# Where the last four scale sums of the opening are made: on VectorE, or on GpSimd and ScalarE

## The chip, the core and the metric

The kernel runs on one core of one Trainium2 chip. The metric is the device time of one execution in microseconds (us). The engines are named as in the profile: PE is TensorE (PEld its weight loads), DVE is VectorE, ACT is ScalarE, POOL is GpSimd, SP is SyncE, whose queue issues the DMAs.

## The reference

One transformer-like block on x (2048 tokens x 1024 channels, f32), modulated by a condition vector c:

```
mod = (silu(c) @ w_mod) in six rows of 1024: sa, ca, ga, sb, cb, gb
h = layernorm(x) * (1 + ca) + sa
x = x + ga * infini_attention(h)      # 32 heads, 4 segments of 512 tokens, wq wk wv wo, memory
h = layernorm(x) * (1 + cb) + sb
x = x + gb * token_mlp(h)             # layernorm, w1 (2048 -> 3584), gelu, w2 (3584 -> 2048)
```

The change touches only how ca, the first scale row, is summed: ca[n] is the sum over k of silu(c)[k] * w_mod[k, 1024 + n].

## The kernel before, in words

The work has four stages: an opening (the first 53 us or so), the attention over 64 steps of (pass, group of four heads, segment), the output projection with the second modulation, and the token MLP in two large products of matrices. Matmuls with f32 accuracy are made as three products of a high part (a cast, L123 or L125) and a low part (the rest, L126), both held in one "page".

The opening works on segment 0 and goes over eight chunks `ct` of 128 channels (lines 278 to 298). Each chunk needs a shift column sa and a scale column 1 + ca, which stand per partition in the tile `saca`. For both, a tile `wm` (128 x 1024) of w_mod is loaded (L281, eleven buffers). The shift's tile is transposed in memory beforehand, so that silu(c), spread over all partitions in `scb`, is multiplied along the free axis and summed by one VectorE operation with an accumulator (L283). The scale's tile is treated in two ways. For chunks 0 to 3 (`NSC = 4`) it lies untransposed and eight small matmuls with one column each sum it on TensorE (L291). For chunks 4 to 7 it lies transposed as the shift's does; two GpSimd products of 512 columns (L287) write wm times scb in place and one ScalarE copy with an accumulator sums it (L288). VectorE then adds 1 (L295).

With both columns, `h_chunk` makes the chunk of h: four TensorE transposes of the normalised x tiles into a PSUM bank (L223), a ScalarE evacuation with scale and shift (L225), a high part (on ScalarE for segment 0, L123; on VectorE for later segments, L125) and a low part (on GpSimd for segment 0, on GpSimd or VectorE for later ones, L126). `first_chunk` multiplies the finished page by the first weights (L196 for k and v, twelve matmuls; L204 for q, three), one chunk behind `h_chunk`.

Beside it, segment 1 is prepared: its four x tiles are queued on SP behind the last `wm` (`issue_after(last_wm)`, L573), VectorE takes their statistics (L131) and ScalarE normalises them (L218). Then come the evacuation of the first products (L358 to L366), segment 1's eight `h_chunk`s (line 577), and the projections of the second step (lines 578 to 581). From there on each step's pieces are laid out by the loop of lines 630 to 653.

What sets the order: the program's text gives each engine's instructions, but the order on each engine is planned at build. Line 1053 asks the tile framework to schedule with a timed simulation of the program, so the durations it assumes for the operations enter into the order. The profile shows that order: saca of chunk 4 stands ahead of saca of chunk 3 on VectorE (L295, both near 35.5 us), and the matmuls with high parts stand ahead of those with low parts on TensorE. Each engine then runs its list in that order, waiting by semaphores. Tiles of the opening share memory with tiles of later stages, which wait for their release.

Of the kernel before, what the change touches and what calls it, by code (L numbers as in the profile page):

```python
# [12 lines left out]
AF = mybir.ActivationFunctionType  # L13
ALU = mybir.AluOpType
# [33 lines left out]
def attention_and_mlp(ctx, tc, x, wq, wkv, wo, beta, w1, b1, w2, b2, c, wm_a, wm_b, out):  # L48
    nc = tc.nc
    V, A, G, T, SY = nc.vector, nc.scalar, nc.gpsimd, nc.tensor, nc.sync  # L50
# [18 lines left out]
    scb, gaw = (a.tile([P, D], F32, name=n) for n in ("scb", "gaw"))  # L69
# [94 lines left out]
    def load_part(g, pr, kind, part, res):  # L164

        if pr == 0:
            split_part(g, kind, part, fetch_part(g, kind, part))
            return
        for i in range(2):
            w = aw.tile([P, 2, 512], F32R, tag="w", bufs=8, name=f"w{kind}{pr}_{g}_{part}_{i}")  # L170
            SY.dma_start(w.bitcast(F32), wsp[g, 2 * part + i if kind == "v" else 4 + i])
            res[kind, 2 * part + i] = w
# [47 lines left out]
    def h_chunk(pool, xs, seg, ct):  # L220
        ps = bank(*(("s1", 2), ("s2", 2))[ct % 2] if seg else ("s2", 2), f"hps{seg}_{ct}")
        for i in range(4):
            T.transpose(ps[:, 128 * i:128 * i + 128], xs[i][:, P * ct:P * ct + P], ident)  # L223
        h32 = pool.tile([P, L], F32, tag="h32", bufs=HB, name=f"h32_{seg}_{ct}")
        A.activation(h32, ps, AF.Identity, scale=saca[:, ct, 1:2], bias=saca[:, ct, 0:1])  # L225
        pg = new_page(f"h{seg}_{ct}")
        split(pg, h32, V if seg else A, V if seg and ct % 2 else G)
        hpages[seg, ct] = pg
# [38 lines left out]
    def first_chunk(ct):  # L267
        h = hpages[0, ct]
        for half in range(2):
            kv_chunk(W[0, 0], h, half, ct, two_tiles(first[half]))  # L270
        q_chunk(W[0, 0], h, ct, first[2])
# [5 lines left out]
    scs = s1p.tile([P, NK], F32, name="scs")  # L277
    for ct in range(NK):
        for part in range(2):
            wm = s1p.tile([P, D], F32, tag="wm", bufs=11, name=f"wm{ct}_{part}")  # L280
            last_wm = SY.dma_start(wm, wm_a[part, ct])  # L281
            if part == 0:
                V.scalar_tensor_tensor(wm, wm, 1.0, scb, op0=ALU.mult, op1=ALU.mult, accum_out=saca[:, ct, 0:1])  # L283
            elif ct >= NSC:
                for i in range(2):
                    c = slice(512 * i, 512 * i + 512)
                    G.tensor_tensor(wm[:, c], wm[:, c], scb[:, c], op=ALU.mult)  # L287
                A.activation(wm, wm, AF.Copy, accum_out=scs[:, ct:ct + 1])  # L288
            else:
                for k in range(NK):  # L290
                    T.matmul(scale_ps[:, ct:ct + 1], wm[:, P * k:P * k + P], sc[:, k:k + 1], start=(k == 0),  # L291
                             stop=(k == NK - 1), skip_group_check=True)
        if ct < 3:
            load_part(0, 0, *(("v", 0), ("q", 0), ("v", 1))[ct], W[0, 0])
        V.tensor_scalar_add(saca[:, ct, 1:2], (scale_ps if ct < NSC else scs)[:, ct:ct + 1], 1.0)  # L295
        h_chunk(s1p, xs[0], 0, ct)
        if ct:
            first_chunk(ct - 1)
# [331 lines left out]
    for n in range(-LEADS, 4 * NI + VL):  # L630
# [11 lines left out]
        if 59 <= m < 67:  # L642
            seg, ct = 2 + (m - 59) // 4, 2 * ((m - 59) % 4)
            reload_h(seg, ct)
            reload_h(seg, ct + 1)
        if 4 * NI - 5 <= m < 4 * NI + 3:
            i = m - 4 * NI + 5
# [409 lines left out]
```

## Time and profile before

| | us |
|---|---|
| median of three runs | 2281.92 (2280.88 to 2282.4) |
| the profiled execution | 2281.25 |
| its span, first to last instruction | 2279.5 |
| mean granted TensorE clock | 0.989 of full speed |

| engine | busy in the first 54 us | busy in the span |
|---|---|---|
| PE | 39.63 | 2214.7 |
| DVE | 33.70 | 1671.9 |
| ACT | 32.76 | 1148.1 |
| POOL | 32.03 | 735.6 |

How to read the lines that follow. A timeline row has start, duration, engine, line, operation, output tile, input tiles, shapes and count; in brackets stand the idle time ahead of it and what ended it. A row of the chain of waits has start, duration, engine, tile and line. A row of the waits has who waited for whom, then the total, the number of times and the longest. A row of a group ends with busy time, mean nanoseconds of one, and idle time ahead by releaser. A row of one tile's or line's instructions has minimum, median and maximum duration in nanoseconds, and the first and last start. A row of a window has the stretch, its length, the busy time and the count of PE, PEld, DVE, ACT and POOL, then the granted TensorE clock (1.00 is full), the DMA engines' share and GB/s.

### The profile page before, as it was taken

The page shows a single profiled execution, that of the slowest core. Times are in us where ns is not written, and L with a number is a line of the kernel's source. Part 1 is how long each engine was busy: PE and PEld are TensorE (multiplying, and loading weights), DVE is VectorE, ACT ScalarE, POOL GpSimd, SP SyncE. Part 2 cuts the span into 40 slices and gives each one's busy share as a digit, 9 for nine tenths or more (in the row PEclk, how much of TensorE's full clock was granted, in tenths as well). Part 3 has the DMA queues.
Part 4 walks back from the last instruction along what each step waited for, and adds up shares of the span by engine and source line. Part 5 has one row for each costly group of instructions (what it writes and reads, how often), then busy time and mean ns, then how long its engine had stood idle before and what let it go on. Part 6 is the DMA issues. An engine that isn't in the chain of part 4 may idle for free.

```text
span 2279.5 us, 38372 instructions
## 1 busy us (share of the span) xinstructions
PE 2214.7 (97%) x13802; PEld 1905.5 (84%) x13802; DVE 1671.9 (73%) x3798; ACT 1148.1 (50%) x2090; POOL 735.6 (32%) x843
## 2 busy tenths in 40 slices
PE   7999999999999999999999999999999999999999
PEld 6888898888988889987877887888887888888887
DVE  6676677766777677664878555788889787878787
ACT  6476677665666666654646333533334242424232
POOL 5165566655766666644000000023333000000000
PEclk9999999999999999999999999999999999999999
DMA  6656565687567566673455765556557441414134
GB/s 259 202 170 172 145 192 167 188 265 230 167 189 209 171 193 185 210 245 108 138 197 201 273 239 194 218 198 235 208 203 277 162 153 56 153 56 143 56 120 148
DMA packets 172882, 415.72 MB, mean 182 GB/s; under 512 B 17268, under 2 KB 71572, under 8 KB 163732
## 3 DMA queue, kind: packets, MB, share of 16 engines
q1 hardware_dynamic: 172692, 413.27, 55.3%
q8 instruction: 110, 1.80, 0.3%
q14 instruction: 80, 0.66, 0.1%
HBM read 237.28 MB, written 125.06 MB: 159 GB/s over the span
## 4 chain that ended last, share of the span: by engine, by line
PE 80%; DMA 7%; DVE 7%; ACT 3%; POOL 2%; issue 1%; SPq 0%; DVEq 0%; ACTq 0%; POOLq 0%
PE mx L849 39%; PE nps L196 13%; PE qps L204 8%; PE po L734 6%; PE pv L504 4%; DMA xb<-x1d 2%; DMA x1e<-xb 2%; PE a L475 1%; PE sx L440 1%; PE sz L440 1%; PE rd L412 1%; DMA sk<-nt 1%; PE a L478 1%; DVE xb L906 1%; PE up L422 1%
## 5 line engine op out<-in xcount | busy, mean ns | idle before, releaser
L849 PE MATMUL mx<-bU,sp 128*128 128x512 f32 x2352 | 535.4, 389 | 3.0 <-DVE sp L126 1.7
L849 PEld LDWEIGHTS mx<-bU,sp 128*128 128x128 f32 x2352 | 441.0, 188 | 96.9 <-DVE sp L126 2.7
L123 ACT CAST sp<-wr 128x384 fp32r<-128x384 f32 (+2 forms) x408 | 217.0, 545 | 451.7 <-PE mx L849 373.7
L196 PE MATMUL nps<-wv,h 128*128 128x256 f32 x3072 | 436.5, 283 | 3.5 <-POOL h L126 3.5
L849 PE MATMUL mx<-bA,sp 128*128 128x512 f32 x1764 | 434.4, 392 | 5.5 <-ACT sp L123 3.3
L490 POOL TENSOR_TENSOR ph<-p,ph 128x640 f16<-128x640 f32 x256 | 377.3, 1495 | 153.7 <-ACT ph L488 153.5
L196 PEld LDWEIGHTS nps<-wv,h 128*128 128x128 f32 x3072 | 404.5, 190 | 10.4 <-POOL h L126 4.7
L849 PEld LDWEIGHTS mx<-bA,sp 128*128 128x128 f32 x1764 | 332.9, 189 | 76.4 <-ACT sp L123 4.4
L126 DVE TENSOR_TENSOR sp<-wr,sp 128x384 fp32r<-128x384 f32 (+2 forms) x408 | 258.1, 643 | 32.0 <-ACT sp L123 31.9
L856 DVE TENSOR_TENSOR ac<-mx,ac 128x512 f32<-128x512 f32 x280 | 189.3, 685 | 92.8 <-PE mx L849 92.3
L204 PE MATMUL qps<-h,wq 128*128 128x512 f32 x768 | 199.9, 406 | 2.3 <-DVE pv L507 1.1
L734 PE MATMUL po<-wo,ots 128*128 128x512 f32 x768 | 183.8, 395 | 6.6 <-DVE more_x L737 2.8
L488 ACT CAST ph<-p 128x1280 f16<-128x1280 f32 x128 | 161.2, 1260 | 44.7 <-POOL p L486 44.1
L734 PEld LDWEIGHTS po<-wo,ots 128*128 128x128 f32 x768 | 144.3, 190 | 38.0 <-ACT ots L123 2.7
L441 DVE CUSTOM_DVE_ANT_0 sx<-sx,mask 128x128 f32<-128x128 f32 (+1 forms) x256 | 109.8, 429 | 86.5 <-PE sx L440 85.1
L204 PEld LDWEIGHTS qps<-h,wq 128*128 128x128 f32 x768 | 144.0, 194 | 31.3 <-issue 2.8
L849 PE MATMUL mx<-bB,sp 128*128 128x512 f32 x588 | 164.0, 389 | 0.0
L486 POOL TENSOR_SCALAR_AFFINE_SELECT p<-p 128x256 f32<-128x256 f32 x256 | 119.5, 475 | 125.3 <-ACT p L479 65.9
L504 PE MATMUL pv<-vp,ph 128*128 128x97 bf16 (+1 forms) x2560 | 144.1, 203 | 1.6 <-DVE red L511 1.3
L504 PEld LDWEIGHTS <-ph 128*128 128x128 f16 x2560 | 115.3, 99 | 25.4 <-issue 12.9
L849 PEld LDWEIGHTS mx<-bB,sp 128*128 128x128 f32 x588 | 110.5, 188 | 23.1
L856 DVE TENSOR_TENSOR cc<-mx,cc 128x512 f32<-128x512 f32 x140 | 94.2, 682 | 37.5 <-PE mx L849 37.2
(208 smaller groups left out, 3208.3 us busy)
## 6 DMA issues: line engine op xcount, KB each, us to landing
sk<-sg SPq DMA_DIRECT2D x384, 128.0 KB
wr<-in_w_dram SPq DMA_DIRECT2D x28, 1024.0 KB
wr<-in_w_dram SPq DMA_DIRECT2D x32, 768.0 KB
bstu<-ucd SPq DMA_DIRECT2D x28, 768.0 KB
wsp<-wv SPq DMA_DIRECT2D x32, 512.0 KB
rawm<-in_wm_b_dram SPq DMA_DIRECT2D x32, 512.0 KB
wv<-wsp SPq DMA_DIRECT2D x32, 512.0 KB
pcd<-cc SPq DMA_DIRECT2D x14, 1024.0 KB
```

Of the source, the lines that this page charges most:

```text
L123: A.copy(hi, src)
L126: lo_eng.tensor_tensor(lo, src, hi.bitcast(F32), op=ALU.subtract)
L196: T.matmul(ps[:, aa], h[:, j, 128 * tt:128 * tt + 128], wt[:, i, o:o + 256], start=(n == 0), stop=(n >= 6 * NK - 2), skip_group_check=True)
L204: T.matmul(ps, wt[:, i, o:o + 128], h[:, j], start=(k + n == 0), stop=(3 * k + n == 3 * NK - 1))
L441: marks[4 * t + h - LEADS, "V"] = V.tensor_tensor_reduce(o, o, mask[:, 384 - 128 * i:], 1.0, -3.0e38, op0=ALU.add, op1=ALU.max, accum_out= ...
L486: G.affine_select(w, w, pattern=[[0, 2], [1, 128]], compare_op=ALU.is_ge, fill=0.0, base=0, channel_multiplier=-1)
L488: marks[n, "A"] = A.copy(ph[:, 0], p32)
L490: marks[n, "G"] = G.tensor_tensor(ph[:, 1, c], p32[:, c], ph[:, 0, c], op=ALU.subtract)
L504: T.matmul(pv[:, i, 0:w], ph[:, part, o:o + 128], d["vp"][:, j, h, 0:w], start=(n == 0), stop=(n == 19), skip_group_check=True)
L734: T.matmul(ps, os_[:, i, P * ct:P * ct + P], wop[ct, nh][:, j], start=(n == 0), stop=(n == 3 * NK - 1))
L849: T.matmul(ps, ops[q][:, i, P * k:P * k + P], b[:, j], start=(m == 0 and first), stop=(m == 3 * nk - 1), skip_group_check=True)
L856: V.tensor_tensor(d, ps, d, op=ALU.add)
```

## The change

For chunks 4 to 7, the two GpSimd products and the ScalarE sum are replaced by one VectorE operation that multiplies and sums, in the form that the shift sums have. Loads, layouts, buffers and everything behind `scs` stay.

```diff
             elif ct >= NSC:
-                for i in range(2):
-                    c = slice(512 * i, 512 * i + 512)
-                    G.tensor_tensor(wm[:, c], wm[:, c], scb[:, c], op=ALU.mult)
-                A.activation(wm, wm, AF.Copy, accum_out=scs[:, ct:ct + 1])
+                V.scalar_tensor_tensor(wm, wm, 1.0, scb, op0=ALU.mult, op1=ALU.mult, accum_out=scs[:, ct:ct + 1])
```

## The prediction

> **What bounds the kernel now.** First the page's engine shares, then what PE waited for in the opening (28 to 72 us), then the chain of waits through that stretch, then the timelines of single engines.
>
> ```profile
> PE 2214.7 (97%) x13802; PEld 1905.5 (84%) x13802; DVE 1671.9 (73%) x3798; ACT 1148.1 (50%) x2090; POOL 735.6 (32%) x843
> ```
>
> PE is busy 97% of the span, so work taken off POOL or ACT in the steady part gives nothing. The opening differs. The waits of PE there:
>
> ```profile
> PE nps L196 <- POOL h L126: 3.5, 4, 1.4
> PE hps L223 <- ACT x L218: 0.8, 1, 0.8
> PE hps L223 <- ACT h L225: 0.8, 1, 0.8
> PE hps L223 <- DVE sg L126: 0.7, 1, 0.7
> PE kps L372 <- DVE r L365: 0.4, 1, 0.4
> ```
>
> The largest is four waits for POOL's low part of an h page. The chain says why POOL is late:
>
> ```profile
> 31.70 5.00 POOL wm L287 x4
> ...
> 37.20 1.73 POOL h L126
> ...
> 42.40 1.23 POOL h L126
> 43.63 2.49 POOL wm L287 x2
> 46.12 1.24 POOL h L126
> ...
> 47.40 1.21 PE nps L196 x8
> ...
> 53.32 0.34 ACT k L358
> ...
> 55.02 1.13 ACT x L218
> ```
>
> From 31.7 to 47.4 us the chain alternates between the h pages' low parts and the products that the change removes (L287); only at 47.4 does PE take it over, until the last first_chunk ends at 53.3. Then ACT's evacuation follows, and with it the last normalised x tile of segment 1 (55.02). PE's own rows:
>
> ```profile
> 38.99 1.19 PE L196 MATMUL nps<-wv,h 128*128 128x256 f32 x8 [0.23 <-POOL h L126]
> ...
> 43.68 1.21 PE L196 MATMUL nps<-wv,h 128*128 128x256 f32 x8 [1.45 <-POOL h L126]
> ...
> 47.40 1.21 PE L196 MATMUL nps<-wv,h 128*128 128x256 f32 x8 [1.34 <-POOL h L126]
> ...
> 49.62 1.11 PE L196 MATMUL nps<-wv,h 128*128 128x256 f32 x8
> ...
> 51.73 1.11 PE L196 MATMUL nps<-wv,h 128*128 128x256 f32 x8
> ...
> 56.21 0.55 PE L223 MATMUL hps<-ident,x 128*128 128x128 f32 x3 [0.84 <-ACT x L218]
> ```
>
> Chunks that don't wait are 51.73 - 49.62 = 2.1 us apart; those that wait lose 0.23, 1.45 and 1.34.
>
> **What goes and what comes.** The groups of the stretch 28 to 54 us, all engines:
>
> ```profile
> L287 POOL TENSOR_TENSOR wm<-wm,scb 128x512 f32<-128x512 f32 x8 | 11.0, 1407 | 0.0
> ...
> L225 ACT ACTIVATE h<-hps,saca 128x512 f32<-128x512 f32 x6 | 4.5, 771 | 3.9 <-DVE saca L295 3.9
> L288 ACT ACTIVATE wm<-wm 128x1024 f32<-128x1024 f32 x4 | 4.2, 1058 | 6.7 <-POOL wm L287 6.7
> L123 ACT CAST h<-h 128x512 fp32r<-128x512 f32 x6 | 3.6, 616 | 0.1
> ...
> L134 ACT ACTIVATE mv<-mv,eps 128x1 f32<-128x1 f32 x4 | 1.2, 290 | 0.3 <-DVE mv L133 0.3
> ...
> L135 ACT ACTIVATE mv<-mv 128x1 f32<-128x1 f32 x4 | 0.8, 198 | 0.1
> ```
>
> POOL loses eight products, 11.0 us. ACT loses four sums, 4 x 1.06 = 4.2 us, and the short reads behind them. DVE gains four operations like those of the shift sums, whose price and surroundings are these:
>
> ```profile
> L283 DVE SCALAR_TENSOR_TENSOR wm<-wm,scb x8: 1209/1216/2284, 12.7 to 38.3; 128x1024 f32<-128x1024 f32 x8
> ```
> ```profile
> 29.38 1.22 DVE L283 SCALAR_TENSOR_TENSOR wm<-wm,scb 128x1024 f32<-128x1024 f32 x1
> 30.53 0.08 DVE L283 DVE_READ_ACCUMULATOR wm<-wm,scb 128x1 f32 x1
> 35.44 0.15 DVE L295 TENSOR_SCALAR saca<-scs 128x1 f32<-128x1 f32 x1 [4.83 <-ACT wm L288]
> ```
>
> One takes 1.22 us alone and up to 2.28 beside POOL. I take 4 x 1.22 = 4.9 us of DVE time; the bounds are 4.9 and 4 x 2.28 = 9.1. I take the low end because what stretched them was POOL's two-input work, most of which goes. The cover is DVE's idle 4.83 us ahead of 35.44, where it waits for ACT's sum of chunk 4: that wait is itself a part of what goes.
>
> [...]
>
> **Does DVE become late instead?** Of the tiles for chunks 4 to 7, six operations remain after 30.6 us (two shift sums, four scale sums): 6 x 1.22 = 7.3 us, ending at 37.9. The data are there in time:
>
> ```profile
> 28.00:38.00 10.00, 10.00 (x69) 9.47 (x68) 4.97 (x10) 4.83 (x8) 7.59 (x6) 1.00 1.02 408
> 38.00:48.00 10.00, 6.97 (x49) 5.81 (x48) 6.51 (x17) 7.30 (x17) 10.00 (x8) 1.00 0.18 70
> ```
>
> The transfers end near 38 + 10 x 70/408 = 39.7 us, and the four x tiles queued behind the last wm take 4 x 0.524 MB at 408 GB/s = 5.1 us, so the last wm lands at about 34.6 (an estimate from these two rows). The SP queue issues the same loads from the same buffers in the same order; the last five wait for tiles of chunks 0 to 2, which the change leaves alone. No DMA is added. After saca of chunk 7 come 0.77 + 0.62 us on ACT and 1.2 to 1.3 on POOL (the chain's 1.23 and 1.24). With PE's transposes at 37.0 as now, ACT is through chunks 4 to 7 at 38.1 + 4 x 1.39 = 43.7 and POOL at 45.0, while PE reaches the low part of chunk 7 at 51.73 - 3.0 = 48.7. Even with all six at 2.28 us, DVE ends at 44.3 and POOL's page is ready near 47.2. So PE is late next, with its own 2.1 us a chunk.
>
> **The sum.** *Term 1*, PE's three waits for POOL: 0.23 + 1.45 + 1.34 = 3.0 us; the end of the chunks goes from 53.3 to 50.3. Bounds 0 and 3.5 (with the fourth wait, the rest of that row of waits).
>
> *Term 2*, the last x tile of segment 1 (ACT, 55.02 to 56.15). The segment's own operations:
>
> ```profile
> L131 DVE BATCH_NORM_STATS2 st<-x x8: 637/678/683, 39.9 to 48.6; 128x6 f32<-128x512 f32 x8
> L218 ACT ACTIVATE x<-x,mv x4: 1227/1228/1273, 49.8 to 54.9; 128x1024 f32<-128x1024 f32 x4
> ```
>
> Behind 38.1 ACT has 5.6 us for h pages, four normalisations at 1.23 and 1.2 + 0.8 of small operations (L134, L135): 12.5 us, so it could finish near 50.6, 0.3 us behind the chunks' end where it is now 2.85 behind. What else waits there (the 0.8, 0.7 and 0.4 of the first fence) stays, since it follows the evacuation. I take the 1.1 us of the chain's own piece; bounds 0 and 2.7 (0.84 + 0.82 + 0.66 + 0.42, all four).
>
> *Term 3*, the clock:
>
> ```profile
> 53.30:58.00 4.70, 2.78 (x21) 1.90 (x18) 1.87 (x4) 4.70 (x12) 1.82 (x8) 1.00 0.00 0
> 58.00:62.00 4.00, 3.18 (x17) 3.12 (x17) 3.72 (x6) 3.68 (x7) 1.28 (x1) 0.57 0.67 141
> ```
>
> After the thin stretch (PE 2.78 of 4.7 us) TensorE is granted 0.57 for 4 us: 0.43 x 4 = 1.7 us lost. With less waiting the spell may shorten or go; bounds 0 and 1.7, and I take the middle, 0.9.
>
> Sum 3.0 + 1.1 + 0.9 = 5.0 us off the profiled execution's 2281.25: **2276.2 us**. (That execution is 0.67 below the median of 2281.92 and inside the three runs.) All bounds together: 0 to 7.9 us, 2273.3 to 2281.25. Behind the opening PE is full (452 of 460 us in a row below), so what is won stays unless the later order changes.
>
> **The rivals.** *The gate stays at x.* DVE has the four new operations ahead of segment 1's statistics (L131). If the order fixed at build puts the statistics as late as now, or POOL's remaining low parts stretch them, the last x tile still ends near 56 and the 3.0 us of term 1 become waiting for it. For it: DVE starts these statistics between 39.9 and 48.6 now, and DVE alone gets more work. Against it: DVE idles 4.83 us ahead of 35.44 for ACT's sum, and is busy only 6.51 of the 10 us from 38 to 48. Time 2280.5; it decides if the last L218 ends later than about 55.
>
> *The order of later work turns out worse (slower).* The order on each engine is fixed at build by a timed plan, so other costs in the opening can reorder work far behind it. What an order is worth shows in two stretches of the same attention work:
>
> ```profile
> 100.00:540.00 440.00, 420.21 (x3591) 379.97 (x3590) 303.87 (x898) 299.25 (x560) 260.76 (x302) 0.96 0.63 187
> 540.00:1000.00 460.00, 452.15 (x4012) 414.03 (x4011) 322.52 (x1003) 291.83 (x518) 304.61 (x372) 1.00 0.64 188
> ```
>
> The first loses 19.8 us idle and 0.04 x 440 = 17.6 us of clock, the second 7.9 and almost none. The losses come in spells of half clock:
>
> ```profile
> 132.00:142.00 10.00, 9.69 (x41) 7.74 (x40) 7.25 (x21) 8.62 (x15) 6.47 (x9) 0.66 0.90 277
> 258.00:268.00 10.00, 7.60 (x22) 5.93 (x23) 6.82 (x21) 5.18 (x10) 5.38 (x5) 0.66 0.27 107
> ```
>
> A spell costs 0.34 x 10 + 0.31 = 3.7 us in the first row and 0.34 x 10 + 2.40 = 5.8 in the second, mean 4.75. One more cancels the gain; three more give 2276.2 + 14.3 = 2290.5. It decides from two more spells on. For it: the first stretch, with several spells, begins close behind the opening. Against it: a shift of everything by the same few microseconds keeps the order, and a spell may as well vanish (one fewer: 2276.2 - 4.75 = 2271.5).
>
> [...]
>
> **How the numbers follow.** 0.2% is 4.6 us, about what a measurement of this kernel can tell from no change: under 2277.4 is faster, over 2286.5 slower. Forecast 0.50 (0.42 of it faster, 0.08 within the bound, where term 2 or 3 fails); the gate at x 0.20, within the bound; the later order 0.30 (0.28 slower, 0.02 within). Together faster 0.42, same 0.30, slower 0.28. The likeliest case alone spans 2273 to 2279. The range reaches down to all bounds won and a spell less at the cheap price (2273.3 - 3.7 = 2269.6) and up to the later order: **2270 to 2291**.
>
> **What would show it.** Right: no wait of PE for POOL's h pages between 38 and 50 us; the last saca of the opening near 38, ahead of the statistics; the last first_chunk near 50.3; the last L218 near 51; the shift of 4 to 5 us still there at 100, 540 and 1000 us. Term 1 is wrong if PE waits there for DVE or ACT instead; term 2 if hps still waits for x; term 3 if the granted clock behind 55 is as low for as long. The sum as a whole is wrong if the shift at 100 us is right and the one at 1000 us isn't.

## The result, and the profile after

The changed kernel takes 2297.6 us (median of six runs, 2294.36 to 2301.1) against 2282.15 us for the kernel before beside it: ratio 1.0067, 95% interval 1.0055 to 1.008, so 15 us slower. The forecast was 2276.2 us, within 2270 to 2291. The profiled execution has a span of 2295.5 us, 16.0 more than before. In the changed kernel's profile every line behind the change has a number that is 3 lower.

First TensorE's waits and rows of the opening, the counterparts of those shown for before:

```profile
PE up L419 <- DVE pk L390: 2.0, 1, 2.0
PE hps L223 <- ACT x L218: 1.5, 2, 1.2
PE nps L196 <- POOL h L126: 0.7, 2, 0.3
```
```profile
41.83 1.21 PE L196 MATMUL nps<-wv,h 128*128 128x256 f32 x8 [0.35 <-POOL h L126]
...
47.57 1.55 PE L196 MATMUL nps<-wv,h 128*128 128x256 f32 x12
48.95 0.85 PE L204 MATMUL qps<-h,wq 128*128 128x512 f32 x3
...
52.83 0.55 PE L223 MATMUL hps<-ident,x 128*128 128x128 f32 x3 [1.25 <-ACT x L218]
...
57.54 2.10 PE L419 MATMUL up<-v,pk 128*128 128x132 f32 x8 [1.99 <-DVE pk L390]
...
70.29 4.39 PE L196 MATMUL nps<-wv,h 128*128 128x256 f32 x35 [0.34 <-POOL h L126]
```

The waits for POOL fell from 3.5 to 0.7 us, and the last first_chunk ends at 49.8 us instead of 53.3. But the lead is gone twenty microseconds later: TensorE waits 1.25 us for a normalised x tile and 1.99 for `pk`, and the last low part of segment 1 reaches it at 70.29 us, where it was 69.21 before.

The four new operations cost what the rows of before said:

```profile
L285 DVE SCALAR_TENSOR_TENSOR wm<-wm,scb x4: 1215/1215/1224, 29.2 to 39.4; 128x1024 f32<-128x1024 f32 x4
```

So the opening accounts for 1 us of the 16. The other 15 are lost further on, most of them hundreds of microseconds behind the change. Before, then after, in two stretches of the attention:

```profile
100.00:600.00 500.00, 478.78 (x4114) 434.32 (x4113) 345.94 (x1028) 338.68 (x630) 296.63 (x346) 0.97 0.64 189
600.00:1000.00 400.00, 393.59 (x3489) 359.68 (x3488) 280.44 (x875) 252.40 (x448) 268.74 (x329) 1.00 0.63 186
```
```profile
100.00:600.00 500.00, 473.93 (x4068) 429.02 (x4067) 345.51 (x1010) 334.94 (x623) 294.89 (x342) 0.97 0.62 188
600.00:1000.00 400.00, 388.79 (x3429) 354.25 (x3428) 277.43 (x860) 247.92 (x439) 266.28 (x322) 0.98 0.60 177
```

From 100 to 600 us TensorE idles 4.9 us more at the same granted clock; from 600 to 1000 it idles 4.8 us more, and the clock is 0.98 instead of 1.00. The clock goes in three spells that the kernel before doesn't have between 600 and 1000 us. They cost another 6.6 us (0.42 x 8 + 0.38 x 4 + 0.43 x 4). Here they are, with the granted clock third from the right:

```profile
664.00:672.00 8.00, 6.60 (x30) 4.64 (x30) 5.88 (x16) 4.84 (x10) 7.13 (x7) 0.58 0.01 2
760.00:764.00 4.00, 3.63 (x10) 2.85 (x11) 4.00 (x12) 1.87 (x3) 3.22 (x4) 0.62 0.25 69
822.00:826.00 4.00, 3.94 (x15) 3.01 (x16) 2.59 (x8) 1.68 (x3) 1.81 (x5) 0.57 0.95 350
```

No instruction there was touched. What differs is the order: compared as built, 7355 of TensorE's 13578 matmuls stand at another place in its list (135 of them in the opening, 7220 behind it), though the program gives TensorE exactly the same instructions.

### The profile page after: what moved, and what is told of

The parts are those of the page before. It is cut to its first block, busy times and chain, and to the rows that moved or that the text cites. A ratio compares the mean times of both kernels' runs of the same rounds, so it can differ in the third digit from the quotient of the medians.

```text
span 2295.5 us, 38358 instructions
## 1 busy us (share of the span) xinstructions
PE 2220.4 (97%) x13802; PEld 1907.9 (83%) x13802; DVE 1680.5 (73%) x3806; ACT 1144.6 (50%) x2082; POOL 728.7 (32%) x835
## 4 chain that ended last, share of the span: by engine, by line
PE 76%; DMA 9%; DVE 7%; ACT 3%; issue 2%; POOL 2%; SPq 1%; DVEq 0%; POOLq 0%; ACTq 0%
PE mx L846 39%; PE nps L196 12%; PE qps L204 8%; PE po L731 4%; PE pv L501 3%; DMA xb<-x1d 3%; DMA x1e<-xb 2%; PE a L472 1%; PE sx L437 1%; DMA sk<-nt 1%; POOL ph L487 1%; PE up L419 1%; PE sz L437 1%; PE rd L409 1%; DVE xb L903 1%
## 5 line engine op out<-in xcount | busy, mean ns | idle before, releaser
L204 PE MATMUL qps<-h,wq 128*128 128x512 f32 x768 | 202.6, 410 | 1.2 <-DVE r L362 1.1
L485 ACT CAST ph<-p 128x1280 f16<-128x1280 f32 x128 | 160.9, 1258 | 47.0 <-POOL p L483 46.8
L204 PEld LDWEIGHTS qps<-h,wq 128*128 128x128 f32 x768 | 146.2, 197 | 31.2 <-DVE r L362 1.2
```

Source lines behind the costliest of these rows:

```text
L204: T.matmul(ps, wt[:, i, o:o + 128], h[:, j], start=(k + n == 0), stop=(3 * k + n == 3 * NK - 1))
L485: marks[n, "A"] = A.copy(ph[:, 0], p32)
```

## The experiments

Theories: LATER ORDER, the cost comes from the order that the build's plan gives to work behind the opening; OPERATIONS, it comes from the new VectorE operations and what they delay. To tell them apart, operations and order were taken from different kernels. The order of a kernel as built was written out, engine by engine, and laid onto the other as edges of issue order, which add no wait:

```diff
+def pinned(tc):
+    ...
+    for e, packed in ORDER.items():
+        rows = np.cumsum(np.frombuffer(zlib.decompress(base64.b85decode(packed)), dtype=np.int16).astype(int))
+        for p, q in zip(rows[:-1], rows[1:]):
+            tc.add_manual_dep(own[e][q], own[e][p].name, mybir.DependencyInfo(
+                mybir.DependencyClass.NoSync, mybir.DependencyReason.DATA), reason="order")
...
         attention_and_mlp(ctx, tc, **args)
+        pinned(tc)
```

Ratios below are against runs of the kernel before on the same chip (medians 2279 to 2281 us there), with the 95% interval.

**The control: before, with its own order pinned.**

> The kernel before, with its own order of every engine written out as edges of issue order (no waits added). A control for the three kernels beside it. Theory LATER ORDER (the 15 us come from the order that the plan gives to work behind the opening) and theory OPERATIONS (they come from the four new VectorE operations and what they delay in the opening) both expect the time of before: 2282, within 2 us. If it is more than 4 us away, the edges themselves cost time and the other three can't be read.

Measured: 2280.51 us, ratio 1.0005 (0.9994 to 1.0016). The edges cost nothing that shows.

**The changed operations and opening, then the order of before.**

> The changed kernel with its own order in the opening (up to the second step's k transposes, some 75 us) and, behind it, every engine in the order of the kernel before. LATER ORDER: the opening ends 1.1 us later than before (the last low part of segment 1 reaches TensorE at 70.29 instead of 69.21 us), the rest is as before: 2283, 2280 to 2286. OPERATIONS: stays near 2297.

Measured: 2281.31 us, ratio 1.0008 (0.9998 to 1.0018). All four new operations are there, and the loss is gone. OPERATIONS falls.

**The reverse: before's operations and opening, then the changed kernel's order.**

> The kernel before with its own opening and, behind it, every engine in the order of the changed kernel. LATER ORDER: 2297.6 - 1.1 = 2296.5, 2293 to 2300. OPERATIONS: near 2282.

Measured: 2299.67 us, ratio 1.0089 (1.0074 to 1.0105). The loss, without the change. The same waits appear at the same places. Around 760 us, the changed kernel's timeline of PE (first) and this one's (its line numbers are 7 higher, for L204 4):

```profile
758.95 0.36 PE L501 MATMUL pv<-vp,ph 128*128 128x65 bf16 x6 [0.65 <-POOL ph L487]
760.37 4.85 PE L204 MATMUL qps<-h,wq 128*128 128x512 f32 x13 [1.06 <-DVE r L362]
```
```profile
757.55 0.36 PE L508 MATMUL pv<-vp,ph 128*128 128x65 bf16 x6 [0.66 <-POOL ph L494]
758.98 6.16 PE L208 MATMUL qps<-h,wq 128*128 128x512 f32 x19 [1.07 <-DVE r L369]
```

The pair of waits (0.65 and 1.06, 0.66 and 1.07 us) belongs to the order, whatever operations made the opening.

**The changed operations with the order of before from the start.**

> The changed kernel with the order of the kernel before on all engines from the start; only on VectorE the shift sums, scale sums and columns of the opening stand in the changed kernel's order, ahead of segment 1's statistics. LATER ORDER, with the gain of the opening as forecast in terms 1 and 2: 2282 - 2.5 (term 1 or 2, whichever ends last) = 2279.5, 2276 to 2282, no wait of PE for POOL's h pages between 42 and 50 us. OPERATIONS: near 2297.

Measured: 2279.02 us, ratio 0.9998 (0.9989 to 1.0007): between 2.5 us faster and 1.6 slower, the expected 2.5 at the very edge. Its opening went as expected (line numbers 4 above those of before):

```profile
42.23 1.21 PE L200 MATMUL nps<-wv,h 128*128 128x256 f32 x8
...
46.56 1.11 PE L200 MATMUL nps<-wv,h 128*128 128x256 f32 x8
...
48.67 1.11 PE L200 MATMUL nps<-wv,h 128*128 128x256 f32 x8
49.62 0.63 PE L208 MATMUL qps<-h,wq 128*128 128x512 f32 x2
...
53.69 0.55 PE L227 MATMUL hps<-ident,x 128*128 128x128 f32 x3 [0.84 <-ACT x L222]
```

No wait for POOL is left, the last chunk's low part starts at 48.67 instead of 51.73, and the transposes behind the last x tile start at 53.69 instead of 56.21, 2.5 us earlier. At the first evacuation of segment 1's k, 2.1 us of the lead are left (69.08 us instead of 71.16). That much the change does bring in the opening with an order that suits it; in the whole time it is too little to be resolved.

**One operation alone, TensorE's order unchanged.** Chunk 4's scale sum only:

```diff
+            elif ct >= NSC and (ct == 4):
+                V.scalar_tensor_tensor(wm, wm, 1.0, scb, op0=ALU.mult, op1=ALU.mult, accum_out=scs[:, ct:ct + 1])
             elif ct >= NSC:
```

> Only chunk 4's scale sum by VectorE, chunks 5 to 7 as before. The plan then gives TensorE and the SP queue exactly the order of the kernel before: one of the four operations alone, without another order. OPERATIONS (the new VectorE operation itself costs): a quarter of the loss, 2282 + 4 = 2286. LATER ORDER: 2282 within 2 us, since POOL's chain of chunks 5 to 7 still bounds the opening.

Measured: 2279.57 us, ratio 1.0001 (0.9988 to 1.0013). The operation itself costs nothing that shows.

**Another order, without any of the operations.** A copy that nobody reads:

```diff
+        if ct == 6:
+            V.tensor_copy(bc[:, 0:4], bc[:, 4:8])
         V.tensor_scalar_add(saca[:, ct, 1:2], (scale_ps if ct < NSC else scs)[:, ct:ct + 1], 1.0)
```

> The kernel before with one more VectorE copy of 128x512 in the opening, ahead of chunk 6's column, into a tile that nobody reads any more: about 0.4 us of VectorE's idle time, none of the change's operations. The plan puts 7579 of TensorE's 13578 matmuls at other places (7355 with the change). OPERATIONS: 2282. LATER ORDER: not 2282 but what this order happens to give. If the order of before was a favourable one (FAVOURABLE), 2288 to 2300; if that of the changed kernel was an unfavourable one among many (UNFAVOURABLE), anywhere from 2276 to 2290.

Measured: 2291.3 us, ratio 1.0047 (1.003 to 1.0064). The copy costs some 11 us. It didn't run as expected, in idle time ahead of chunk 6's column: the plan put it among the statistics of the first x tiles, and it took 0.69 us:

```profile
7.95 0.69 DVE L296 COPY bc<-bc 128x512 f32<-128x512 f32 x1
```

But the opening loses nothing by it. The first evacuation of segment 1's k, before (first) and here, starts at the same time:

```profile
71.16 0.37 ACT L358 COPY k<-nps 128x256 f32<-128x256 f32 x1 [3.97 <-PE nps L196]
```
```profile
71.19 0.37 ACT L360 COPY k<-nps 128x256 f32<-128x256 f32 x1 [2.66 <-PE nps L196]
```

So the 11 us are lost behind it, where no instruction is new and only the order differs.

**Chunks 4 and 5, then chunk 6 alone,** with `(ct < 6)` and `(ct == 6)` in the condition shown above:

> Chunks 4 and 5 by VectorE, 6 and 7 as before; 5465 matmuls moved. OPERATIONS: half the loss, 2290. LATER ORDER: whatever its order gives: 2288 to 2300 with FAVOURABLE, 2276 to 2290 with UNFAVOURABLE; not in proportion to the number of operations.

> Chunk 6 alone by VectorE; 7515 matmuls moved. OPERATIONS: a quarter of the loss, 2286. LATER ORDER: as for two operations, 2288 to 2300 with FAVOURABLE, 2276 to 2290 with UNFAVOURABLE.

Measured: two operations 2279.35 us, ratio 1.0001 (0.9991 to 1.0012); one operation 2306.1 us, ratio 1.0117 (1.0096 to 1.0137). One costs 27 us and two cost none: nothing here goes with the number of operations. The slow one is ahead at that evacuation of k (70.22 us, before 71.16) and loses its 27 us behind it. Neither reading of what orders cost was right throughout. Of the four other orders tried (changed kernel, copy, two operations, one), three are slower by 11 to 27 us and one is level with before, so the order of before is a good one, but not alone; 2306 lies above both ranges.

The rows of the slowest kernel and of a level one, from 600 to 1000 us (first the one with chunk 6, then the changed operations and opening with the order of before):

```profile
600.00:1000.00 400.00, 384.94 (x3387) 353.56 (x3386) 277.04 (x843) 241.53 (x431) 258.71 (x315) 0.97 0.61 178
```
```profile
600.00:1000.00 400.00, 390.88 (x3442) 356.01 (x3441) 278.54 (x867) 250.82 (x443) 265.58 (x325) 1.00 0.64 188
```

The slow order loses twice: more idle time (15.1 us against 9.1 here) and, with it, clock (0.97 against 1.00).

**Where in the order.** Two kernels with before's operations and opening take the changed order up to the fifteenth step, or from it on. (The attention has 32 steps, two passes of eight groups and two segments, not the 64 named at the start.)

> The kernel before with its own opening, then the changed kernel's order up to the end of the fifteenth attention step (some 580 us), then the order of before. PLACES (the loss belongs to the places where the changed order leaves PE waiting; by hundreds of us, idle time plus clock lost from 100 to 600 us is 37.3 in the profile of before and 41.1 in that of the changed kernel): 3.8 us slower than before. CARRIED (what is lost behind 600 us follows from how the earlier part left the buffers and transfers): the whole 12 us or so, or none.

> The other half: the order of before up to the end of the fifteenth step, then the changed kernel's. PLACES: from 600 to 1000 us 6.4 us are lost in the profile of before and 18.2 in that of the changed kernel, so 11.8 us slower than before, with half-clock spells near 665, 760 and 822 us as in the changed kernel. CARRIED: the other of none and the whole.

Measured: up to it 2287.69 us, ratio 1.0021 (1.0006 to 1.0037), 4.8 us by the ratio (7.2 by the medians); from it on 2296.82 us, ratio 1.0072 (1.0052 to 1.0091), 16.4 us. Together 21, as the whole order gave (20). CARRIED falls. PLACES had the shares about right and the second size low: 11.8 was expected, the interval starts at 11.9. The second kernel shows the three spells where the changed kernel has them, and the same wait ahead of the middle one (L208 and L369 are L204 and L365 of before):

```profile
660.00:668.00 8.00, 7.10 (x36) 5.32 (x37) 5.25 (x15) 3.56 (x6) 7.24 (x8) 0.57 0.01 2
756.00:760.00 4.00, 4.00 (x12) 3.17 (x11) 3.84 (x9) 1.24 (x2) 2.91 (x5) 0.58 0.47 146
818.00:822.00 4.00, 4.00 (x18) 3.19 (x17) 2.14 (x7) 1.68 (x3) 1.36 (x5) 0.57 0.81 244
```
```profile
755.38 6.24 PE L208 MATMUL qps<-h,wq 128*128 128x512 f32 x19 [1.06 <-DVE r L369]
```

**What stays open.** Which engine's order carries the loss was not tried: all five were swapped together. Why the plan picks a worse order is open too; the runs show only what the orders cost.

## Why the prediction was wrong, step by step

The step that failed is the one behind the sum, "what is won stays unless the later order changes", together with the argument against the rival, "a shift of everything by the same few microseconds keeps the order". The order did change, in more than half of TensorE's places, and with it came 13 to 20 us (13 from the changed kernel against the same operations on the old order, 1.0067 and 1.0008; 20 from the reverse swap, 1.0089). The rival of the later order named the mechanism, half-clock spells (granted 0.57 to 0.62 in the three rows above) and idle time in the attention. It also said three spells, and between 600 and 1000 us there are three; as no reason was given for three, that is luck. It was given 0.28 where it was what happened. Its price of 14.3 us was close to the 15 that were lost behind the opening, though made up otherwise: less clock for each spell and more plain idle time (4.9 + 4.8 in the rows above). But that price was set on top of a gain of 5.0 us, and in the changed kernel the opening brought a loss of 1.1. That is why the measured time lies above the upper end.

*Term 1* was right: 3.0 us forecast, and the chunks' end moved from 53.3 to 49.8. With the order of before it moved to 50.25 (49.62 + 0.63 in the rows of that experiment), where 50.3 was forecast. One wait for POOL of 0.35 us stayed in the changed kernel where none was expected. VectorE was in time, as worked out, but 2.7 us later than reckoned (its last sum ends at 40.6 us, not 37.9). Its rows in the changed kernel show why:

```profile
30.58 2.12 DVE L283 SCALAR_TENSOR_TENSOR wm<-wm,scb 128x1024 f32<-128x1024 f32 x1
...
34.74 0.16 DVE L292 TENSOR_SCALAR saca<-scale 128x1 f32<-128x1 f32 x1 [0.90 <-PE scale L288]
...
37.36 2.12 DVE L283 SCALAR_TENSOR_TENSOR wm<-wm,scb 128x1024 f32<-128x1024 f32 x1
```

Two shift sums started while POOL made low parts of h (29.79 to 31.61 and 36.51 to 38.39 us), work that the change leaves, and took 0.9 us longer each (2.12 us against 1.22); another 0.9 went to a wait for TensorE's sum of chunk 3.

*Term 2* failed. In the changed kernel the outcome is that of the rival called the gate at x, a last x tile behind 55 us, but not for its reason: the statistics were not as late as before, they end at 46.8 us instead of 49.2. ScalarE's rows show what held the tile back:

```profile
48.58 0.37 ACT L355 COPY k<-nps 128x256 f32<-128x256 f32 x1 [1.77 <-PE nps L196]
...
49.38 1.26 ACT L218 ACTIVATE x<-x,mv 128x1024 f32<-128x1024 f32 x1
...
51.49 1.28 ACT L218 ACTIVATE x<-x,mv 128x1024 f32<-128x1024 f32 x1
...
53.10 1.29 ACT L218 ACTIVATE x<-x,mv 128x1024 f32<-128x1024 f32 x1
...
56.37 1.28 ACT L218 ACTIVATE x<-x,mv 128x1024 f32<-128x1024 f32 x1
```

ScalarE was free, as reckoned, but its list now has the evacuations between the normalisations: it stands idle 1.77 us for TensorE at the first, and the last x tile is done at 57.65 us instead of 56.15. That idle time was no use to the x tiles, which all stood behind the waiting instruction. With the order of before the term didn't come either. There three normalisations stand ahead of the evacuations and the fourth behind them:

```profile
50.79 0.35 ACT L359 COPY k<-nps 128x256 f32<-128x256 f32 x1
...
52.36 1.27 ACT L222 ACTIVATE x<-x,mv 128x1024 f32<-128x1024 f32 x1
```

The last x tile is done at 53.63 us, 2.5 us earlier than before, but the chunks end 3.1 us earlier, so the tile is 3.4 us behind them where it was 2.85. The 2.5 us come from term 1; of term 2's 1.1 us nothing was won.

*Term 3* had the wrong sign. The spell of the opening grew. From 54 to 62 us, before, the changed kernel, and the changed operations with the order of before:

```profile
54.00:62.00 8.00, 5.26 (x30) 4.31 (x29) 5.60 (x9) 7.68 (x15) 2.40 (x7) 0.79 0.33 71
```
```profile
54.00:62.00 8.00, 5.75 (x27) 4.77 (x28) 4.09 (x10) 5.75 (x10) 0.90 (x2) 0.57 0.59 127
```
```profile
54.00:62.00 8.00, 6.60 (x34) 6.05 (x32) 7.24 (x10) 5.74 (x10) 2.70 (x2) 0.58 0.65 138
```

The clock is 0.57 and 0.58 instead of 0.79: (0.79 - 0.57) x 8 = 1.8 us more of clock lost where 0.9 were to be won, also where TensorE was busier.

*The price of the new operation* was right: all four rows are 1.215 to 1.224 us, where 1.22 was taken.

## What to carry to other kernels

Where a build plans the order from assumed durations, an edit in one place can be an edit of the order everywhere behind it, and the local gain (2 to 3 us here) is small against what another order costs (0 to 27 us here). Price that spread ahead of the edit, as a likely case and not as a tail (three of four other orders were slower here); compare the orders as built, since they tell whether anything moved; and judge the edit itself with the order held fixed. And before counting an engine's freed time as a gain, look at what stands ahead of the work in its list (here an evacuation, for which ScalarE stood idle 1.77 us).

## What the runs showed of the hardware that was not expected

TensorE's clock halved behind waits that were each short (0.52 to 1.15 us). The row of 760 us, with 0.62, follows waits of 0.65 and 1.06 us; that of 822 us, with 0.57, follows waits of 1.15, 0.52 and 1.09. In the changed kernel's 4 us ahead of each the clock is still 1.00, and TensorE is busy for 2.44 and 1.49 us:

```profile
756.00:760.00 4.00, 2.44 (x26) 1.62 (x25) 4.00 (x10) 1.47 (x6) 3.86 (x3) 1.00 0.37 126
818.00:822.00 4.00, 1.49 (x19) 1.19 (x19) 4.00 (x11) 2.57 (x7) 3.28 (x2) 1.00 0.82 279
```

Within the two spells, from 762 to 764 and from 823 to 825 us, the granted clock is 0.50. What sets a spell off was not tried by itself.
